# A searched list order that knows PSUM banks, and a prefetch hint for the last branch, in a fused linear-attention and gated-MLP kernel

## The chip, the cores and the metric

The kernel runs on one core of one Trainium2 chip. The time is device microseconds of one execution of the whole kernel, the median of three runs. Engines are named as in the profile: PE (matrix products; PEld is its weight load), DVE, ACT, POOL, and SP, which here only issues transfers.

## What is computed

The reference is a linear attention with decaying state, followed by a gated MLP with spatial mixing, all in float32, with B=4, H=8, S=768, D=48:

```python
for t in range(S):                                     # attention
    cur = einsum('bhd,bhe->bhde', u[None] * kt, vt)
    y[:, :, t] = einsum('bhd,bhde->bhe', rt, state + cur)
    state = wt[:, :, :, None] * state + einsum('bhd,bhe->bhde', kt, vt)
x = y.transpose(0, 2, 1, 3).reshape(B, S, H * D)       # 4 x 768 x 384
h = gelu(x @ w_in)                                     # tanh form
u, v = h[..., :512], h[..., 512:]
v_n = (v - mean(v)) / sqrt(var(v) + 1e-6) * g_ln
v_s = einsum('ts,bsd->btd', w_sg, v_n) + b_sg[None, :, None]
return x + (u * v_s) @ w_out
```

## The kernel before

The sequence is cut into 24 chunks, four batches of six chunks of 128 steps. For each chunk the kernel scans the decays on DVE (lines 635 to 650), scales the keys (`decayed_k`, 652 and 679), forms the weights of a step's own key (`own_weights`, 691 to 717, whose last part is a group of eight ACT rows at L715 or one product at L717 on DVE or POOL), takes scores on PE into the PSUM bank pair `a_ps` (L740), masks them (`masked`, L817), advances the state (`state`, 831 to 847; `decayed`, four ACT rows at L858 or one product at L860) and gathers the outputs in the PSUM pair `y_ps` (763, 774). `taken` then copies two parts of `y_ps` out: three heads' worth into `x` (128x384) and the fourth into `y` (128x128), both through the helper `copy` at L446, on ACT or on DVE; `move` (L982) sends the `y` rows to their place in `x` by three transfers on SP's queue; `split_x` turns `x` on PE (1003, 1004) and splits it into a high and a low part (`xT`). Most products are run as three, high by high, high by low, low by high (L1014 to L1016).

The MLP runs in pieces of the same work: `v_piece` and `u_piece` (x @ w_in, gelu at L1037 and L1070, layernorm 1039 to 1056), `gate_piece` (spatial mixing with `wsgh`, `wsgl` and 1092 to 1098) and `out_piece` (L1116, with the store at L1118). Weights are loaded and split by `f64_weight` (1158 to 1188) and `f32_weight` (1206 to 1212). The first gate product can only start when all six v pieces of a batch are done, some 75 us into the run; before that, chunks and weight work fill PE. Where PE would be idle early, matmuls on unused data are put in (`warm` and `fill`, L551).

All this is written as procedures that yield an operation at a time. A class `Plan` simulates the engines in Python, with a cost in microseconds for each operation, picks what comes next on which engine, and the kernel emits instructions in that order. What it picks is steered by tables of numbers (`LEAD`, `FIRST`, `PIECE`, `WEIGHT`, `BIAS`, `TOL`, `SHIFT`, `LEAN`, `AHEAD`): a rank for each call of each procedure, and a lean to one engine. An operation's earliest start is the latest of its inputs, its buffers, its engine, and a port shared by DVE and POOL. The emitted order is fixed; on the chip each engine runs its own list and waits on semaphores.

At the end a flag that the checks of range have written is read on each engine (L1292), and `with tc.If(flag > 0)` (L1294) holds a general, slower path, which does not run on these inputs: each engine branches over it. L1464 is the end of the function.

Of the kernel before, what the change touches and what calls it, by code (L numbers as in the profile page):

```python
# [36 lines left out]
LEAD = (12.4645, -2.59387, -4.21285, -7.90312)  # L37
FIRST = {"v": -1.41961, "u": 28.6546, "gate": 10.0262, "out": 26.6142}
PIECE = {"v": -16.9089, "u": 12.3224, "gate": 14.337, "out": 5.856}
WEIGHT = {"v": -13.2274, "u": -50.6824, "sg0": -3.39001, "sg1": -8.4941, "out": 2.71291}  # L40

BIAS = {"DVE": 0.278468, "POOL": 0.125302}
TOL = {"ACT": 0.187321, "DVE": 0.0774238, "PE": 0.0750297, "POOL": 0.0114098, "SP": 0.02}
OWN = {"ACT": 0.12, "DVE": 0.12, "PE": 0.0, "POOL": 0.1}
SHIFT = {
    "f64_weight": {1: -2.65682, 2: -0.0161277, 3: 0.0312938, 4: 7.52904, 5: 8.2742, 6: 0.872807, 7: 2.80997,
        8: 0.987471, 9: 2.80075},
    "f64_check": {0: 0.144801, 1: -0.144084, 2: -0.567729, 3: -0.298354, 4: -0.901301, 5: -0.796411, 6: -1.40305,
        7: -4.54019, 8: -6.21746, 9: -2.35678},
    "range_check": {0: -5.99366, 1: -1.89263, 2: -3.53632, 3: -4.15958, 4: -3.59754, 5: -3.76383, 6: -6.85461,  # L50
        7: -7.08113, 8: -3.31642, 9: -10.4712, 10: -2.92299, 11: 0.109737},
    "f32_weight": {0: -3.99499, 1: -0.0910659, 2: 0.252904, 3: -0.00610032, 4: 0.827835, 5: -1.04847},
    "columns": {0: 0.0800858},
    "consts": {0: -1.42278},
    "load_kr": {0: -0.357877, 1: -0.588202, 2: -0.327565, 3: 0.576721, 4: -0.213968, 5: 0.282151, 6: 0.072508,
        7: -0.109793, 8: -0.0751895, 9: -0.848467, 10: -0.0803527, 11: 0.123607, 13: -1.36602, 14: -1.37566,
        15: -1.37566, 16: -0.255794, 17: -0.423447, 18: 0.00265044, 19: 1.42131, 20: 0.396438, 21: 2.56083,
        22: 4.00369, 23: 0.995513},
    "load_v": {0: 2.55696, 1: 0.24433, 2: 0.29339, 3: -3.53162, 4: -0.539967, 5: 1.43151, 6: 1.21722, 7: 1.33442,
        8: -0.963013, 9: 0.685624, 10: 0.16795, 11: -0.752937, 12: 0.336987, 13: 0.680041, 14: 1.11277,  # L60
        15: -0.819155, 16: 0.412499, 17: 0.652678, 18: -4.10874, 19: -1.39921, 20: -0.196712, 21: -2.95851,
        22: -0.225999, 23: -0.122174},
    "decays": {0: 0.290652, 1: 3.36975, 2: -0.337977, 3: 0.287929, 4: -0.550312, 5: -0.458788, 6: -0.107544,
        8: 0.186735, 9: -0.131388, 10: -0.076173, 11: 0.0119462, 12: 2.29576, 13: 6.35672, 14: 0.74578, 15: 4.6382,
        16: 0.256563, 17: 0.173431, 18: -7.30487, 19: -4.8291, 20: -1.76844, 21: -5.70158, 22: -1.11423,
        23: 0.554462},
    "decayed_k": {0: -1.94935, 1: -0.0499885, 2: -3.469, 3: -4.52965, 4: 1.46376, 5: 1.08007, 6: 1.74482,
        7: 1.82159, 8: -6.25161, 9: 0.461373, 10: -0.258781, 11: -1.05508, 12: 0.0573206, 13: 6.34316,
        14: 0.0715837, 15: -3.39515, 16: -0.550587, 17: 3.31994, 18: 2.03045, 19: 1.63861, 20: 2.50708,
        21: 3.49938, 22: 0.149994, 23: -5.18727},  # L70
    "own_weights": {0: -0.99264, 1: -2.30837, 2: -1.40861, 3: 0.124313, 4: 0.939737, 5: 1.08277, 6: 0.689459,
        7: 0.194852, 8: -0.0430578, 9: 1.36362, 10: 0.628226, 11: 1.72692, 12: 0.453539, 13: 1.31489, 14: 0.36321,
        15: 0.326257, 16: 0.527571, 17: -1.51186, 18: -1.02775, 19: -0.416129, 20: -0.985823, 21: 0.0128711,
        22: 0.414581, 23: 0.751683},
# [12 lines left out]
    "turned": {0: -0.36366, 1: 7.62663, 2: 4.98126, 3: 0.412257, 4: 1.31616, 5: 1.44751, 6: -1.90445, 7: -1.89447},
    "scores": {0: -9.60454, 1: -1.60519, 2: 0.00907207, 3: -1.402, 4: -0.278773, 5: -0.377053, 6: -3.00215,
        7: 0.568393},
    "products": {0: 2.53405, 1: -0.218746, 2: 0.641708, 3: 0.0789209, 4: -0.63387, 5: -1.14758, 6: -2.83415},  # L90
    "outputs": {0: 0.272463, 1: 3.35994, 2: -4.09238, 3: 0.997477, 4: -1.80195, 5: -7.63104},
    "load_w": {1: 0.0390948, 2: -0.314065, 3: 0.528507, 4: -0.0361462, 5: 0.0962989, 6: 0.034904, 7: -0.126869,
        8: -0.418661, 9: -0.623567, 10: -0.635585, 11: -0.171762, 12: 1.00086, 13: 0.0732159, 14: -0.722859,
        15: 2.58094, 16: 0.428369, 17: 1.08119, 18: -0.528971, 19: -0.94875, 20: 0.553405, 21: -0.75299,
        22: 0.915889, 23: 15.5269},
    "chunk_pc": {1: -0.0918095, 2: -1.12188, 3: 0.970453, 4: 3.354, 5: 4.35453, 6: -0.563074, 7: -3.79915,
        8: -4.75251, 9: -4.09779, 10: 0.477875, 11: 3.14907, 12: -3.58171, 13: -2.32428, 14: -1.81168,
        15: 0.960833, 16: 1.60902, 17: -0.319454, 18: -6.14497, 19: -0.652345, 20: -4.72639, 21: -0.537364,
# [72 lines left out]
STRETCH = 6  # L171
# [31 lines left out]
class Op:  # L203
# [11 lines left out]
    def port(self, e):  # L215

        return e == "POOL" or e == "DVE" and self.two


class Event:  # L220
    t = None


class Buf:


    def __init__(self, pool, slot):
# [30 lines left out]
class Plan:  # L258
# [55 lines left out]
    def run(self):  # L314
        while True:
            best = {}
            for p in self.procs:
                op = p[3]
# [18 lines left out]
            op = p[3]  # L337
# [1131 lines left out]
```

## Time and profile before

| what | us |
|---|---|
| median of 3 runs | 361.82 (361.63 to 362.58) |
| profiled execution, its own time | 360.56 |
| span of its trace | 358.7 |
| outside the span | 1.86 |

| engine | busy us | share of the span | instructions |
|---|---|---|---|
| PE | 348.8 | 97% | 4495 |
| DVE | 269.5 | 75% | 556 |
| ACT | 208.2 | 58% | 524 |
| POOL | 93.6 | 26% | 154 |

A line of the profile names the line of the kernel, the engine, the operation, what it writes and reads, and the number of such instructions; then the busy time and the mean of one in ns; then how long the engine was idle just before them, and who ended that. One line of code can stand for several engines, as the planner chose. A gap on an engine counts for the whole only where the work that ends last comes through it.

### The profile page before, as it was taken

Reading aid. Unit: us, or ns where it says so; the run is one execution under the profiler, and the core shown is the slowest. Engines: PE = TensorE matmul, PEld = TensorE weight load, DVE = VectorE, ACT = ScalarE, POOL = GpSimd, SP = SyncE. Lnnn points to the kernel's source line nnn. Section 1 sums busy time; section 2 is a strip of 40 time slices with the busy share of each in tenths; the row PEclk is TensorE's granted clock in tenths of the full one; section 3 lists DMA queues with packets and bytes.
Section 4 is the critical chain, followed back from the end, with each engine's and each line's share of the span. In section 5 each row is a group of like instructions: output and inputs, shape, how many; then the busy total and the mean of one; then the engine's idle time right before and its main releaser. Section 6 shows DMA issues by size and latency. Waiting matters only on the chain.

```text
span 358.7 us, 10925 instructions
## 1 busy us (share of the span) xinstructions
PE 348.8 (97%) x4495; PEld 320.4 (89%) x4495; DVE 269.5 (75%) x556; ACT 208.2 (58%) x524; POOL 93.6 (26%) x154
## 2 busy tenths in 40 slices
PE   8998999999999999999999999999999999999993
PEld 7785777899999899899999988999999989999993
DVE  7999999999999989899659879977550425472341
ACT  2769768782535787571214355862467999994110
POOL 8352323214224321224245233231300221100000
PEclk9999999999999999999999999999999999999999
DMA  7989795720465646253277432330487844431002
GB/s 267 372 254 336 238 324 146 232 84 21 145 222 149 221 146 193 92 151 114 62 225 237 149 108 59 126 107 5 152 244 263 289 122 119 132 115 44 24 2 73
DMA packets 26697, 57.06 MB, mean 159 GB/s; under 512 B 3216, under 2 KB 12176, under 8 KB 26640
## 3 DMA queue, kind: packets, MB, share of 16 engines
q1 hardware_dynamic: 26640, 56.29, 49.6%
q8 instruction: 37, 0.61, 0.7%
q14 instruction: 20, 0.16, 0.2%
HBM read 50.37 MB, written 4.72 MB: 154 GB/s over the span
## 4 chain that ended last, share of the span: by engine, by line
PE 85%; DVE 7%; DMA 3%; ACT 1%; issue 1%; SPq 1%; DVEq 0%; ACTq 0%
PE m_ps L1014 19%; PE m_ps L1015 17%; PE m_ps L1016 17%; PE resets L1014 6%; PE resets L1015 5%; PE resets L1016 5%; PE a_ps L740 5%; PE y_ps L763 4%; PE y_ps L774 3%; DMA x<-y 2%; PE y_ps L747 2%; DVE vn L1165 1%; DVE W L635 1%; DVE winl L1171 1%; DVE W L643 1%
## 5 line engine op out<-in xcount | busy, mean ns | idle before, releaser
L1014 PE MATMUL m_ps<-wsgh,vn 128*128 128x384 f32 x144 | 49.5, 344 | 0.0
L1015 PE MATMUL m_ps<-wsgl,vn 128*128 128x384 f32 x144 | 48.7, 338 | 0.0
L1016 PE MATMUL m_ps<-wsgh,vn 128*128 128x384 f32 x144 | 48.7, 338 | 0.0
L1045 POOL TENSOR_TENSOR st<-st,mhalf 128x1 f32<-128x1 f32 x24 | 13.6, 568 | 58.9 <-DVE st L1039 13.4
L1096 ACT CAST g<-m_ps 128x384 fp32r<-128x384 f32 x24 | 11.4, 479 | 29.4 <-DVE m_ps L1094 29.2
L1014 PEld LDWEIGHTS m_ps<-wsgh,vn 128*128 128x128 f32 x144 | 27.0, 188 | 0.6
L1015 PEld LDWEIGHTS m_ps<-wsgl,vn 128*128 128x128 f32 x144 | 27.1, 188 | 0.1
L1016 PEld LDWEIGHTS m_ps<-wsgh,vn 128*128 128x128 f32 x144 | 27.1, 188 | 0.0
L1014 PE MATMUL m_ps<-g,wouth 128*128 128x384 f32 (+1 forms) x80 | 27.0, 337 | 0.0
L1092 DVE SCALAR_TENSOR_TENSOR m_ps<-m_ps,flat 128x384 f32<-128x384 f32 x24 | 14.7, 620 | 15.9 <-PE m_ps L1016 15.8
L1015 PE MATMUL m_ps<-g,wouth 128*128 128x384 f32 (+1 forms) x80 | 26.6, 332 | 0.0
L1016 PE MATMUL m_ps<-g,woutl 128*128 128x384 f32 (+1 forms) x80 | 26.6, 332 | 0.0
L1014 PE MATMUL m_ps<-xT,winh 128*128 128x384 f32 x75 | 26.2, 349 | 0.0
L1015 PE MATMUL m_ps<-xT,winh 128*128 128x384 f32 x75 | 25.4, 338 | 0.0
L1016 PE MATMUL m_ps<-xT,winl 128*128 128x384 f32 x75 | 25.4, 338 | 0.0
L446 ACT COPY x<-y_ps 128x384 f32<-128x384 f32 x21 | 10.0, 478 | 24.3 <-PE y_ps L763 23.8
L1014 PE MATMUL m_ps<-winh,xT 128*128 128x512 f32 x57 | 23.5, 411 | 0.1
L740 PE MATMUL a_ps<-KR 64*64 64x128 f32 (+1 forms) x768 | 22.4, 252 | 1.1 <-DVE S L847 1.0
L1015 PE MATMUL m_ps<-winl,xT 128*128 128x512 f32 x57 | 22.6, 396 | 0.0
L1016 PE MATMUL m_ps<-winh,xT 128*128 128x512 f32 x57 | 22.6, 396 | 0.0
L704 POOL TENSOR_TENSOR RK<-RK,flat 128x384 f32<-128x384 f32 x14 | 14.1, 1010 | 29.8 <-DVE W L635 5.3
L763 PE MATMUL y_ps<-a,vtok 64*64 64x64 f32 x768 | 21.5, 224 | 0.3 <-DMA vtok<-in_vtok 0.2
(195 smaller groups left out, 1014.0 us busy)
## 6 DMA issues: line engine op xcount, KB each, us to landing
KR<-in_kr SPq DMA_DIRECT2D x24, 512.0 KB, 4.8
RK<-in_ktok SPq DMA_DIRECT2D x20, 384.0 KB, 4.3
W<-in_wpad SPq DMA_DIRECT2D x24, 260.5 KB, 3.9
KR<-in_wpad SPq DMA_DIRECT2D x12, 521.0 KB, 3.8
vtok<-in_vtok SPq DMA_DIRECT2D x24, 192.0 KB, 3.7
out<-o SPq DMA_DIRECT2D x21, 192.0 KB, 2.8
vn<-in_w_in SPq DMA_DIRECT2D x6, 512.0 KB, 5.7
KR<-in_w_in SPq DMA_DIRECT2D x6, 512.0 KB, 4.2
```

The lines of the kernel that those rows point to most:

```text
L446: nc.scalar.copy(o, i) if e == "ACT" else engine[e].tensor_copy(o, i)
L704: engine[op.e].tensor_tensor(t[:, 0], t[:, 0], u_bc, ALU.mult)
L740: nc.tensor.matmul(ps_[64 * c_:64 * c_ + 64, j, p * C:p * C + (2 * T if c_ < turn else T)], x.K[rows, at:at + T], r_, start=True, stop=True)
L747: m = behind(m, nc.tensor.matmul(at(c_)[64 * j:64 * j + 64, p // 2, p % 2], x.kt.tile[64 * c_:64 * c_ + 64, j, p * 64:(p + 1) * 64], x.V[6 ...
L763: m = nc.tensor.matmul(place(y, j, q, r, c_), x.V[64 * c_:64 * c_ + 64, h * D - up(p, j):h * D - up(p, j) + 64], x.a.tile[64 * c_:64 * c_ ...
L774: m = behind(m, nc.tensor.matmul(place(y, j, q, r, c_), S2.tile[64 * j:64 * j + 64, 16 + 64 * p - up(p, j):80 + 64 * p - up(p, j)], x.R[64 ...
L1014: nc.tensor.matmul(ps, lh, rh, start=(i == 0), stop=False)
L1015: nc.tensor.matmul(ps, lh, rl, start=False, stop=False)
L1016: nc.tensor.matmul(ps, ll, rh, start=False, stop=(i == n - 1))
L1045: nc.gpsimd.tensor_tensor(rstd, var, c.mhalf, ALU.pow)
L1092: nc.vector.scalar_tensor_tensor(ps, ps, c.g[:, d:d + 1], c.b_bc[:, ts], ALU.mult, ALU.add)
L1096: nc.scalar.copy(gh, ps)
```

## The change

Three things are changed in the planner and one at the end of the kernel.

First, the planner knows a `Bank`: an operation that names banks may not start before every other engine's last access to them has ended. The copies of `taken`, the mask, the state's additions, the copy of the scores' turned part and a small look at `y_ps` name the banks that they read. Second, some costs are set anew (own weights on PE, state and decayed on POOL and ACT, the small layernorm steps on POOL). Third, every number of the tables is another one. Fourth, a hint for the branch at L1294 is asked for on all five engines. Lines after it move by up to 24; L446 becomes L462, L982 becomes L1003, L1294 becomes L1318.

```diff
-    "state": {0: 1.17605, 1: -1.5654, 2: -0.151852, 4: -1.00713, 5: -1.43132, 6: 0.034972, 7: 0.148255,
+    "state": {0: 1.6156, 1: -1.5654, 2: -0.151852, 4: -1.00713, 5: -1.43132, 6: 0.0152658, 7: 0.148255,
...
+class Bank:
+
+
+    def __init__(self):
+        self.t = {}
+
+    def since(self, e):
+        return max((t for k, t in self.t.items() if k != e), default=0.0)
...
-                                            self.lanes[0] if op.kb is not None else 0.0),))
+                                            self.lanes[0] if op.kb is not None else 0.0,
+                                            *(b.since(e) for b in op.banks)),))
...
+            for b in op.banks:
+                b.t[e] = op.seen
...
+    for n, x in enumerate(ch):
+        x.yb, x.ab = ([Bank(), Bank()] for _ in range(2))
+        x.db = ch[n - 1].yb if n > STRETCH else [Bank(), Bank()]
...
-            op = yield Op({"PE": 1.0}, small=True, after=[e_uc], take=[m_m], free=[rk], n=16)
+            op = yield Op({"PE": 1.3}, small=True, after=[e_uc], take=[m_m], free=[rk], n=16)
...
-        op = yield Op({"DVE": 0.64}, after=[x.e_A, x.e_Sc], done=x.e_M)
+        op = yield Op({"DVE": 0.64}, after=[x.e_A, x.e_Sc], done=x.e_M, banks=x.ab)
...
-            op = yield Op({"DVE": 0.27}, after=[x.e_Ds, x.e_S2], take=[s_S1])
+            op = yield Op({"DVE": 0.27}, after=[x.e_Ds, x.e_S2], take=[s_S1], banks=x.db[:1])
...
-        op = yield Op({"DVE": 0.3, "POOL": 0.6, "ACT": 1.0}, after=[before.e_S1, x.e_pc], take=[s_S2], done=x.e_S2,
+        op = yield Op({"DVE": 0.3, "POOL": 0.49, "ACT": 0.95}, after=[before.e_S1, x.e_pc], take=[s_S2], done=x.e_S2,
...
-        op = yield Op({"ACT": 0.42, "DVE": 0.47}, after=[x.e_ym], take=[s_x] if first else [], apart=True)
+        op = yield Op({"ACT": 0.42, "DVE": 0.47}, after=[x.e_ym], take=[s_x] if first else [], apart=True,
+                      banks=x.yb)
...
-        op = yield Op({"ACT": 0.19, "DVE": 0.22}, take=[s_y3] if first else [], free=[y], apart=True)
+        op = yield Op({"ACT": 0.19, "DVE": 0.22}, take=[s_y3] if first else [], free=[y], apart=True,
+                      banks=x.yb[1:])
...
-        yield Op({"POOL": 0.7})
+        yield Op({"POOL": 0.55})
...
+    tc.mark_branch_hint_location(
+        "general", hint="LikelyTaken",
+        engines=[x.engine for x in (nc.sync, nc.vector, nc.tensor, nc.scalar, nc.gpsimd)])
     flag = nc.values_load(bad[0:1, 0:1], min_val=0, max_val=1)
     fast.close()
-    with tc.If(flag > 0):
+    with tc.If(flag > 0, label="general"):
```

What this makes of the order is seen at three places. The first is the start of SP's list, before and after (`W`, `KR` and `u_col` are the first loads).

```order
L1464 UNCONDITIONAL_BRANCH
L600 DMA W_0_81<-in_wpad 128x521
L609 DMA KR_0_83<-in_kr 128x1024
L1217 DMA u_col<-in_ucol 128x32
L600 DMA W_0_82<-in_wpad 128x521
L609 DMA KR_0_84<-in_kr 128x1024
```

```order
L1488 UNCONDITIONAL_BRANCH
L1488 BRANCH_PREFETCH_HINT
L619 DMA W_0_81<-in_wpad 128x521
L628 DMA KR_0_83<-in_kr 128x1024
L619 DMA W_0_82<-in_wpad 128x521
L1238 DMA u_col<-in_ucol 128x32
L628 DMA KR_0_84<-in_kr 128x1024
```

One hint instruction stands right behind the branch into the kernel, on this and in the same way on each of the other four engines; there is none near L1318, where the branch is.

The second place is the fourth chunk's copies out of `y_ps`, some 42 us into the run. On ACT before and then on DVE before (`x_0_111` and `y_0_114` are the two parts of `taken`, `S` the states):

```order
L446 COPY kt_0_103<-m_ps_0_134 128x512
L1037 ACTIVATE v_0_126,st_0_115<-m_ps_0_133 128x512
L446 COPY x_0_111<-y_ps_0_131 128x3x128
L446 COPY pc_0_97<-W_0_82 128x8
L858 ACTIVATE S_0_109<-S_0_104,pc_0_96 128x48 x4
L446 CAST xT_539<-x_0_110 128x3x128
```

```order
L847 TENSOR_TENSOR S_0_104<-a_ps_0_130,S_0_108 128x192
L446 COPY y_0_114<-y_ps_0_131 128x128
L641 RECIPROCAL resets<-W_0_82 128x4
L679 TENSOR_TENSOR KR_0_84<-KR_0_84,W_0_82 128x512
L652 TENSOR_TENSOR KR_0_83<-KR_0_83,W_0_81 128x512
```

And on ACT after:

```order
L462 COPY pc_0_96<-W_0_81 128x8
L734 ACTIVATE a_0_101<-KR_0_83,own_0_92 128x64 x8
L462 CAST wsgh<-g_572 128x2x384
L462 COPY look_0_95<-y_ps_0_131 128x1
L462 COPY kt_0_103<-m_ps_0_133 128x512
L462 COPY pc_0_97<-W_0_82 128x8
L1058 ACTIVATE v_0_126,st_0_115<-m_ps_0_134 128x512
L462 CAST xT_555<-x_0_110 128x3x128
L1062 ACTIVATE junk,st_0_115<-v_0_126,st_0_115 128x512
L462 COPY x_0_111<-y_ps_0_131 128x3x128
L462 COPY y_0_114<-y_ps_0_131 128x128
L877 ACTIVATE S_0_109<-S_0_104,pc_0_96 128x48 x4
```

Both copies of the chunk now stand one behind the other on ACT, and a group of eight L734 rows (L715 of before) stands ahead of them; over the whole run ACT takes all 24 pairs, where DVE took 12 of the `y` copies and 3 of the `x` copies.

The third place is SP's list around the fourth chunk's move (`g` are parts of the mixing weight), before and after:

```order
L982 DMA x_0_110<-y_0_113 32x128 x3
L1206 DMA g_725<-in_w_sgT 128x2x384
L1206 DMA g_727<-in_w_sgT 128x2x384
L609 DMA KR_0_85<-in_kr 128x1024
L609 DMA KR_0_86<-in_kr 128x1024
L617 DMA vtok_0_87<-in_vtok 128x384
L982 DMA x_0_111<-y_0_114 32x128 x3
```

```order
L1003 DMA x_0_110<-y_0_113 32x128 x3
L642 DMA RK_0_91<-in_ktok 128x768
L1227 DMA g_724<-in_w_sgT 128x2x384
L1227 DMA g_731<-in_w_sgT 128x2x384
L1227 DMA g_737<-in_w_sgT 128x2x384
L642 DMA RK_0_90<-in_ktok 128x768
L636 DMA vtok_0_87<-in_vtok 128x384
L628 DMA KR_0_86<-in_kr 128x1024
L1003 DMA x_0_111<-y_0_114 32x128 x3
```

Seven loads instead of five stand between the third move and the fourth.

Counted over each list up to the first gate product, PE has 6 more u products, 16 more scores and 3 fewer fillers, and the rest alike; DVE has 148 rows for 150, ACT 162 for 130, POOL 66 for 59. Of DVE's, one more set of a weight's split (four rows, less one of another set), two more L1052, one L652, one L679 and one L709 come; two L717, one L706, one L840 and six small rows go. Of ACT's, two groups of eight L715, three groups of four L858, three L1070 and one L1041 come, two L1050 go. Over the whole run ACT has 136 L715 rows for 80.

## Rows read from the trace of the kernel before

**Rows 1.** The page: busy time, share and instructions of each engine.

```profile
PE 348.8 (97%) x4495; PEld 320.4 (89%) x4495; DVE 269.5 (75%) x556; ACT 208.2 (58%) x524; POOL 93.6 (26%) x154
```

**Rows 2.** Windows before and behind the first gate product: stretch, its length, then busy times.

```profile
core 0: us, PE busy (x) PEld busy (x) DVE busy (x) ACT busy (x) POOL busy (x), PEclk, DMA share, GB/s
0.00:75.00 75.00, 71.16 (x1081) 57.16 (x1082) 71.25 (x155) 53.29 (x145) 29.12 (x63) 1.00 0.79 260
75.00:345.80 270.80, 270.34 (x3366) 256.15 (x3364) 194.69 (x394) 154.46 (x379) 64.46 (x91) 1.00 0.44 136
```

**Rows 3.** Waits of PE: line <- releaser: us in total, times, longest.

```profile
PE m_ps L551 <- POOL junk L528: 1.2, 1, 1.2
PE a_ps L740 <- DVE S L847: 1.0, 1, 1.0
...
PE m_ps L1003 <- ACT u L1070: 0.4, 1, 0.4
```

**Rows 4.** The chain that ended last, in order of time: start, us, what.

```profile
46.18 5.11 DMA x<-y
...
53.01 0.91 PE m_ps L1003 x2
...
99.84 0.88 PE a_ps L740 x32
```

**Rows 5.** Timeline of the last 6 us: start, us, engine, line, [idle <-releaser].

```profile
353.13 0.36 DVE L1116 TENSOR_TENSOR u<-m_ps,x 128x192 f32<-128x192 f32 x1 [0.76 <-PE m_ps L1016]
353.52 0.46 SPq L1118 DMA_DIRECT2D out<-u  x1
```

**Rows 6.** Transfers issued from 350 us on: KB each, median us to landing.

```profile
out<-u SPq DMA_DIRECT2D x2, 96.0 KB, 1.7
```

**Rows 7.** Instructions of L1294: queue, count, ns min/median/max, first to last start.

```profile
L1294 SPq EVENT_SEMAPHORE  x8: 17/17/17, 356.7 to 357.3; - x8
...
L1294 ACTq COMPARE_BRANCH  x1: 50/50/50, 347.7 to 347.7; - x1
L1294 ACTq EVENT_SEMAPHORE  x1: 17/17/17, 348.2 to 348.2; - x1
L1294 PEldq COMPARE_BRANCH  x1: 3842/3842/3842, 351.2 to 351.2; - x1
...
L1294 SPq COMPARE_BRANCH  x1: 50/50/50, 354.0 to 354.0; - x1
```

**Rows 8.** Timeline: two matmuls of 384 columns in a row on PE.

```profile
345.02 0.34 PE L1016 MATMUL m_ps<-wsgh,vn 128*128 128x384 f32 x1
345.19 0.34 PE L1014 MATMUL m_ps<-wsgh,vn 128*128 128x384 f32 x1
```

**Rows 9.** Groups of instructions by line and shape: busy us, mean ns | idle before.

```profile
L715 ACT ACTIVATE a<-KR,own 128x64 f32<-128x64 f32 x80 | 20.2, 338 | 1.0 <-DVE own L709 0.9
...
L679 DVE TENSOR_TENSOR KR<-KR,W 128x512 f32<-128x512 f32 x22 | 15.8, 721 | 0.2 <-DMA KR<-in_kr 0.2
...
L652 DVE TENSOR_TENSOR KR<-KR,W 128x512 f32<-128x512 f32 x17 | 12.6, 742 | 0.0
...
L858 ACT ACTIVATE S<-S,pc 128x48 f32<-128x48 f32 x40 | 10.1, 324 | 2.3 <-DVE S L847 2.2
...
L1052 DVE TENSOR_SCALAR v<-v,st 128x512 f32<-128x512 f32 x9 | 4.9, 547 | 0.7 <-POOL st L1047 0.5
...
L717 DVE TENSOR_TENSOR a<-own,KR 128x512 f32<-128x512 f32 x7 | 4.8, 679 | 0.0
...
L446 DVE COPY y<-y_ps 128x128 f32<-128x128 f32 x12 | 3.5, 290 | 12.8 <-ACT x L446 12.8
...
L1043 DVE TENSOR_SCALAR st<-st 128x1 f32<-128x1 f32 x22 | 3.1, 142 | 4.5 <-ACT junk L1041 4.5
...
L1165 DVE SCALAR_TENSOR_TENSOR g<-g,g 128x384 int32<-128x384 int32 x4 | 2.1, 555 | 0.0
...
L1163 DVE TENSOR_SCALAR g<-g 128x384 int32<-128x384 int32 x4 | 1.3, 352 | 0.0
```

More of the change, by code (lines that the diff above doesn't have):

```diff
@@ L34 @@
 WMID, WHALF = 1.11, 0.48
[L37 to L43, printed above, removed]
+LEAD = (12.2642, -2.6384, -4.06392, -10.5789)
+FIRST = {"v": -1.82498, "u": 25.5999, "gate": 6.37033, "out": 27.5547}
@@ L44 @@
+PIECE = {"v": -20.0832, "u": 13.1418, "gate": 16.1515, "out": 12.0275}
+WEIGHT = {"v": -13.2138, "u": -47.5409, "sg0": -1.91549, "sg1": -20.2575, "out": 4.3844}
+BIAS = {"DVE": 0.351334, "POOL": 0.115945}
+TOL = {"ACT": 0.147636, "DVE": 0.0774238, "PE": 0.0629901, "POOL": 0.0642896, "SP": 0.02}
 OWN = {"ACT": 0.12, "DVE": 0.12, "PE": 0.0, "POOL": 0.1}
 SHIFT = {
-    "f64_weight": {1: -2.65682, 2: -0.0161277, 3: 0.0312938, 4: 7.52904, 5: 8.2742, 6: 0.872807, 7: 2.80997,
-        8: 0.987471, 9: 2.80075},
@@ L48 @@
[L48 to L62, printed above, removed]
@@ L172 @@
 RESETS = 8
[L173 to L174 removed]
+AHEAD = {"decays": -0.692084, "decayed_k": -8.62155, "own_weights": 13.6876, "masked": -2.18884, "state": 0.2945,
+         "decayed": 21.3635, "taken": -34.7049, "stretch": -4.83707, "move": -5.22689, "split_x": -0.281107}
 HMIN = float.fromhex("0x1.2p-15")
@@ L203, with __init__ @@
 class Op:
-    def __init__(self, on, after=(), take=(), free=(), done=None, kb=None, two=False, apart=False, small=False, slack=0.0, n=6):
+    def __init__(self, on, after=(), take=(), free=(), done=None, kb=None, two=False, apart=False, small=False, slack=0.0, n=6,
+                 banks=()):
         self.on, self.after, self.take, self.free, self.done, self.kb = on, after, take, free, done, kb
         self.two = two
+        self.banks = banks
         self.n = n
@@ L831, in state @@
             nc.vector.tensor_tensor(two(S1.tile), x.ds_at(0), two(values(x.S2.tile)), ALU.add)
-        op = yield Op({"DVE": 0.3, "POOL": 0.6} if g else {"DVE": 0.3}, after=[x.e_Ds, x.e_pc], take=[s_S2], done=x.e_T2,
-                      two=g > 0)
+        op = yield Op({"DVE": 0.3, "POOL": 0.49} if g else {"DVE": 0.3}, after=[x.e_Ds, x.e_pc], take=[s_S2], done=x.e_T2,
+                      two=g > 0, banks=[] if g else x.db[:1])
         (S1 if g else x.ds).done(op.seen)
@@ L842, in state @@
         if not last:
-            op = yield Op({"DVE": 0.27}, take=[s_S1], done=x.e_S1)
+            op = yield Op({"DVE": 0.27}, take=[s_S1], done=x.e_S1, banks=x.db[1:])
             x.S1, = op.got
@@ L873, in outputs @@
         pe_own(x, y, True)
-        op = yield Op({"ACT": 0.1, "DVE": 0.1}, take=[s_look])
+        op = yield Op({"ACT": 0.1, "DVE": 0.1}, take=[s_look], banks=x.yb[:1])
         look, = op.got
@@ L935, in turned_copy @@
         m = T if last_of(n) else C
-        op = yield Op({"ACT": 0.5, "DVE": 0.61}, after=[x.e_T], take=[s_kt], done=x.e_kt)
+        op = yield Op({"ACT": 0.5, "DVE": 0.61}, after=[x.e_T], take=[s_kt], done=x.e_kt, banks=x.ab)
         x.kt, = op.got
@@ L1037, in v_piece @@
         nc.scalar.activation(v, m.tile, AF.Gelu_apprx_tanh, accum_out=neg)
-        op = yield Op({"POOL": 0.3, "DVE": 0.08}, two=True)
+        op = yield Op({"POOL": 0.2, "DVE": 0.08}, two=True)
         engine[op.e].tensor_scalar(neg, neg, -1.0 / FF, None, ALU.mult)
```

196 lines of the change are left out of this document (106 added, 90 removed), and 16 rows, old and new, of the table SHIFT.

## The prediction

> **What bounds the kernel now.** I read the shares of the page first, then the windows, then PE's waits, and only then the chain and the end. PE is busy for 348.8 of 358.7 us, 97% [rows 1], so the whole is PE's work plus the little that PE is idle. The windows say where that little lies [rows 2]: from 75 us, when the first gate product starts, to 345.8 us PE is busy 270.34 of 270.80 us, and in the first 75 us it is busy 71.16, idle 3.84. Whatever an order can win without taking work from PE is therefore in the head, and is at most 3.84 us. PE's longest waits agree: 1.2 us at the very start for data that POOL writes, 1.0 for a state on DVE, 0.4 for a gelu on ACT [rows 3]. In the head DVE is busy 71.25 of 75 us and ACT 53.29 [rows 2]: DVE, not PE, is the fullest engine there, and ACT has 21.7 us to spare. The chain that ended last goes once through a transfer, 5.11 us from 46.18, and is back on PE at 53.01 [rows 4]; this is the fourth chunk's move of `y` into `x`.
>
> The end is a place of its own. The last add on DVE starts at 353.13, the last store is issued at 353.52 [rows 5], and a store of this size lands 1.7 us after its issue [rows 6], so at about 355.2. But SP, which takes its branch at 354.0 in 50 ns, runs its next instruction at L1294 only at 356.7 [rows 7]: 2.7 us later, some 1.5 behind the store's landing. ACT's branch stands at 347.7 and its next instruction at 348.2, 0.45 us later; PE's own branch record is 3.84 us long [rows 7], but it starts at 351.2, and ends at 355.05, ahead of SP. So the branch over the general path costs an engine between some 0.45 and 3.8 us, and on SP it is what ends last. What lies behind it in the span is 358.7 less 356.7, 2.0 us, and stays.
>
> **The change part by part.** *The banks.* Of DVE's waits the largest that a bank order could end is that of the 12 `y` copies, 12.8 us in all, all for the `x` copy on ACT [rows 9]. From the code, the two read the same PSUM pair. With both copies on ACT that wait is gone, and ACT takes the 12 copies at about the 0.29 us that DVE had: 3.5 us over the whole run on an engine that is idle for 358.7 less 208.2 us [rows 1]. PE's list of waits has none for one of these copies, and behind 75 us PE is idle for 0.46 us in all [rows 2]. So nearly all of the 12.8 us were beside PE's work, and I cost the bank part at nothing; what hides it is the dense PE of the second window, and if that cover were gone PE would show idle time there.
>
> *The order of the head.* Ahead of the first gate product PE now does 6 more u products and 16 more scores. Two products of 384 columns follow each other by 0.175 us (345.02 to 345.19) [rows 8], so six are 1.05 us; 16 scores are one piece of 0.88 us [rows 4] (each stands twice in the trace). That is 1.93 us of work that fits into the head and need not be done later. The 3 fillers fewer have no price, since they stand only where PE is idle. Against this stands DVE, the fullest engine of the head, whose list up to that product changes as follows [rows 9]. It gains a weight set less one of its rows (0.352 and twice 0.555: 1.46), two L1052 (1.09), an L679 and an L652 (1.46) and a reduction of 384 columns at the 0.555 of the like-sized L1165 (0.56): 4.57 us. It loses two L717 (1.36), one product of 384 columns (0.56), one state product of 192 columns, which I put at the 0.29 of the `y` copy, and six small rows, between 0.142 and 0.29 each: 0.85 to 1.74, middle 1.30: in all 3.51. DVE's net is +1.06 us, and 0.6 to 1.5 by the bounds. If DVE sets the first gate product's time, that product comes 1.06 us later with 1.93 us more behind it: **-0.87 us, I take -0.8**. By DVE's bounds it is -0.4 to -1.3; if DVE's added rows all fall into its own 3.75 us of idle, -1.9; the ceiling is PE's 3.84.
>
> *The fourth move.* Seven loads instead of five stand between the third move and the fourth on SP's queue. An issue takes SP 0.46 us [rows 5], so two more in front of it are up to 0.9 us, on a chain that passes through this move [rows 4]; the PE work between that chunk's end and the product that the move feeds is shorter by a u triple as well. This is a part of the upper bound of the order and not of its middle, since the copies ahead of it are ordered anew as well.
>
> *The smaller costs* (own weights, state, small POOL rows) change no instruction's time; they act through the order alone and are in the counts above.
>
> *The hint.* It adds one instruction on each engine at the start. The nearest rows, control instructions at L1294, take 17 to 50 ns [rows 7]; SP's first load stands behind it, so +0.05, and up to 0.2 if it holds its queue for four of them. What it may win is at the end: if the code behind the branch is there, SP needs only the landing of the last store. From 356.7 to 355.2 that is **-1.5 us**. Bounds: 0 if the hint does nothing; -1.5 if all engines follow, because then the landing is next in line; between them, since DVE's and PE's branches end at about the same time as SP's, a part. I take -1.5, since the ACT row shows that 0.45 us is enough for a branch on this kernel, which from 354.0 would be before the landing.
>
> [...]
>
> The sum: -0.8 + 0.05 - 1.5 = -2.25 us. Against the profiled execution (358.7 in the span and 1.86 outside of it, 360.56) that is 358.3; the median of the runs stands 1.26 above that execution, and the prediction is for a median: 361.82 - 2.25 = 359.6 (**A**).
>
> **The rivals.** *B: the hint does nothing.* It stands some 350 us ahead of the branch; thousands of instructions run between on PE (4495 rows [rows 1]). Then SP's 2.7 us stay: 361.82 - 0.8 + 0.05 = 361.1. For it: the place of the hint in the order. Against: five instructions that name a branch by its label may hold its place and act when it comes near, and nothing in the trace of before tells. In the same family, a hint that brings code in at a bad time could cost a fetch at the start, priced at PE's 3.84 us [rows 7]: 361.82 - 0.8 + 3.84 = 364.9; I give that little.
>
> *C: ACT becomes the head's bound, and the kernel is slower.* ACT's list ahead of the first gate product grows from 130 to 162 rows. Two groups of eight L715 come at 8 x 0.2525 (20.2 us over 80 rows) = 2.0 us each, three groups of four L858 at 4 x 0.2525 (10.1 over 40) = 1.0 us each [rows 9], so some 7 us and the copies. ACT's 21.7 us of room [rows 2] hide them as long as none stands ahead of a row that PE is waiting for. The place is in the order: a group of L734 now stands three to eight rows ahead of the fourth chunk's copies, and PE already waits 0.4 us for an ACT row in the head [rows 3]. One group in front of one such row costs 2.0 us and decides the head as soon as DVE's list is not later than it: 361.82 + 2.0 + 0.05 - 1.5 = 362.4 with the hint, 363.9 without it. Against it: 21.7 us of room is a lot for 7.
>
> *E: the order takes all of PE's idle time out of the head*, and the hint works: 361.82 - 3.84 - 1.5 + 0.05 = 356.5. For it: a searched order that has 1.93 us more PE work early. Against: 1.2 us of the waits are at the very start, before any data is there.
>
> **How the numbers follow.** Chances: A 0.48, B 0.25, C 0.16 (half of it with the hint), E 0.09, harm by the hint 0.02. The likeliest is A, 359.6. Its own range, by the order's -1.9 to -0.4 and the hint's -1.5 to -0.9, is 358.4 to 360.6. The range of eight in ten reaches to B and to the first of C's times: 357.4 (A's low end less 1 us for a head that is part of the way to E) to 363.0 (C's 362.4 and half a us); left out are E, C without the hint and the harm, 0.19. A measurement of this kernel tells a difference from none at about 0.3%, 1.1 us, so faster is below 360.7 and slower above 362.9. Faster: A and E less a small part of A's upper end, 0.54. Same: B, C with the hint, and that part, 0.36. Slower: C without the hint and the harm, 0.10.
>
> **What would show it.** In the changed kernel's windows, PE's idle time up to the first gate product should be 3 us or less, with the first gate product near 76 us, and behind it PE dense as now. The DVE wait for the `x` copy should be gone without a change of PE's idle time behind the head; if PE's second window gains, the cover that I named was not one. At L1294, SP's next instruction should come about 1.2 us after its branch (the landing) rather than 2.7; if it is still 2.7 the hint is B. PE's branch record, now 3.84 us, should be short if the hint acts on PE. An ACT row in front of a long PE wait in the head would be C. I am wrong altogether if the end is not SP's branch but the runtime's work behind it, or if PE's matmuls themselves change their spacing.

## The result and the profile after

The changed kernel took 357.87 us (357.33 to 358.74, 4 runs) against 361.75 us (361.63 to 362.58, 4 runs) for the kernel before beside it: a ratio of 0.989, 95% interval 0.9864 to 0.9916, or -3.9 us. Forecast were 359.6 us and -2.25. The profiled execution of the changed kernel took 358.19 us, of which the trace spans 356.5; against 360.56 and 358.7 before that is -2.4 and -2.2. Two later series, on two chips and with more runs, gave smaller gains than the first comparison: 0.9954 (0.9936 to 0.9973) and 0.9937 (0.9915 to 0.996), -1.4 and -2.5 us between the medians. The kernel before had 360.03 (35 runs) and 360.75 us (34 runs) there.

The windows of the changed kernel, up to 75 us, on to the last stretch, and the last stretch of PE's work, to be read beside [rows 2] (PEclk is the granted clock, 1.00 for full speed):

```profile
core 0: us, PE busy (x) PEld busy (x) DVE busy (x) ACT busy (x) POOL busy (x), PEclk, DMA share, GB/s
0.00:75.00 75.00, 70.76 (x1075) 56.53 (x1076) 70.56 (x141) 56.88 (x170) 32.87 (x70) 1.00 0.80 266
75.00:345.00 270.00, 269.67 (x3366) 255.71 (x3364) 186.13 (x350) 162.03 (x417) 77.00 (x123) 1.00 0.44 135
345.00:352.30 7.30, 7.29 (x51) 7.08 (x50) 3.17 (x7) 0.48 (x1) 0.00 (x0) 1.00 0.14 46
```

PE's idle time in the head is 4.24 us, where it was 3.84 [rows 2]; behind it PE is as dense as it was. PE's waits, to be read beside [rows 3] (line <- releaser: us, times, longest):

```profile
PE m_ps L567 <- POOL junk L544: 1.3, 1, 1.3
PE m_ps L715 <- POOL RK L710: 0.7, 1, 0.7
PE m_ps L1196 <- ACT winl L462: 0.7, 1, 0.7
```

The 1.0 us for a state on DVE is gone, and a wait of 0.7 us for ACT has come. DVE's `y` copies, which waited 12.8 us for ACT [rows 9], stand on ACT now, and a state's addition on DVE waits for them instead:

```profile
DVE S L850 <- ACT y L462: 7.2, 6, 4.2
```

The timeline of the end, beside [rows 5]:

```profile
352.02 0.27 PE L1037 MATMUL m_ps<-g,woutl 128*128 128x192 f32 x1
352.32 0.36 DVE L1137 TENSOR_TENSOR u<-m_ps,x 128x192 f32<-128x192 f32 x1 [0.76 <-PE m_ps L1037]
352.71 0.53 SPq L1139 DMA_DIRECT2D out<-u  x1
```

The last add starts at 352.32 instead of 353.13, 0.81 us earlier. And the branch, L1318 now, beside [rows 7] (queue, count, ns min/median/max, first to last start):

```profile
L1318 SPq EVENT_SEMAPHORE  x8: 17/17/17, 354.5 to 355.1; - x8
...
L1318 ACTq COMPARE_BRANCH  x1: 68/68/68, 347.0 to 347.0; - x1
L1318 ACTq EVENT_SEMAPHORE  x1: 17/17/17, 347.5 to 347.5; - x1
L1318 PEldq COMPARE_BRANCH  x1: 398/398/398, 350.4 to 350.4; - x1
...
L1318 SPq COMPARE_BRANCH  x1: 70/70/70, 353.3 to 353.3; - x1
```

SP runs on 1.2 us after its branch, at 354.5, which is the store's issue at 352.71 plus 1.8 to its landing; before it was 2.7. PE's branch record is 0.40 us long and was 3.84. From the last add's start to the end of the span it is 356.5 - 352.32 = 4.2 us, and was 358.7 - 353.13 = 5.6: 1.4 us less. The hint instructions at the start took 45 to 56 ns on each engine.

### The profile page after: what moved, and what is told of

It reads as the page before. It is cut to its first block, busy times and chain, and to the rows that moved or that the text cites. A ratio compares the mean times of both kernels' runs of the same rounds, so it can differ in the third digit from the quotient of the medians.

```text
span 356.5 us, 10996 instructions
## 1 busy us (share of the span) xinstructions
PE 347.7 (98%) x4489; PEld 319.3 (90%) x4489; DVE 260.2 (73%) x498; ACT 219.4 (62%) x586; POOL 109.9 (31%) x193
## 4 chain that ended last, share of the span: by engine, by line
PE 87%; ACT 2%; DVE 1%; DMA 1%; issue 0%; SPq 0%; ACTq 0%
PE m_ps L1035 19%; PE m_ps L1037 18%; PE m_ps L1036 18%; PE resets L1035 6%; PE resets L1036 5%; PE resets L1037 5%; PE a_ps L759 5%; PE y_ps L782 4%; PE y_ps L793 3%; PE y_ps L766 2%; DMA x<-y 1%; PE m_ps L1024 1%; PE a_ps L766 1%; ACT a L734 1%; PE m_ps L805 0%
## 5 line engine op out<-in xcount | busy, mean ns | idle before, releaser
L1035 PE MATMUL m_ps<-wsgh,vn 128*128 128x384 f32 x156 | 53.7, 344 | 0.0
L1037 PE MATMUL m_ps<-wsgh,vn 128*128 128x384 f32 x156 | 52.7, 338 | 0.0
L1036 PE MATMUL m_ps<-wsgl,vn 128*128 128x384 f32 x156 | 52.7, 338 | 0.0
L734 ACT ACTIVATE a<-KR,own 128x64 f32<-128x64 f32 x136 | 34.4, 339 | 2.9 <-DVE own L728 2.8
L1035 PEld LDWEIGHTS m_ps<-wsgh,vn 128*128 128x128 f32 x156 | 29.3, 188 | 0.6
L1036 PEld LDWEIGHTS m_ps<-wsgl,vn 128*128 128x128 f32 x156 | 29.3, 188 | 0.0
L1037 PEld LDWEIGHTS m_ps<-wsgh,vn 128*128 128x128 f32 x156 | 29.3, 188 | 0.0
L462 ACT COPY x<-y_ps 128x384 f32<-128x384 f32 x24 | 11.4, 476 | 24.3 <-PE y_ps L782 20.0
L1077 DVE TENSOR_TENSOR vn<-v,vn 128x512 fp32r<-128x512 f32 x24 | 16.9, 706 | 12.3 <-ACT vn L462 10.1
L1035 PE MATMUL m_ps<-xT,winh 128*128 128x384 f32 x69 | 24.3, 352 | 0.0
L1035 PE MATMUL m_ps<-g,wouth 128*128 128x384 f32 (+1 forms) x72 | 24.2, 336 | 0.0
L1036 PE MATMUL m_ps<-g,wouth 128*128 128x384 f32 (+1 forms) x72 | 23.9, 332 | 0.0
L1037 PE MATMUL m_ps<-g,woutl 128*128 128x384 f32 (+1 forms) x72 | 23.8, 331 | 0.0
L725 POOL TENSOR_TENSOR RK<-RK 128x384 f32<-128x384 f32 x16 | 16.1, 1009 | 24.7 <-DVE W L669 6.1
L1036 PE MATMUL m_ps<-xT,winh 128*128 128x384 f32 x69 | 23.3, 338 | 0.0
```

What stands on the lines that cost most here:

```text
L462: nc.scalar.copy(o, i) if e == "ACT" else engine[e].tensor_copy(o, i)
L725: engine[op.e].tensor_tensor(t[:, 1], t[:, 1], t[:, 0], ALU.mult)
L734: nc.scalar.activation(a[:, j, p], eyes, AF.Copy, scale=o[:, j, p:p + 1])
L1035: nc.tensor.matmul(ps, lh, rh, start=(i == 0), stop=False)
L1036: nc.tensor.matmul(ps, lh, rl, start=False, stop=False)
L1037: nc.tensor.matmul(ps, ll, rh, start=False, stop=(i == n - 1))
```

## The experiments

**The hint alone.** The kernel before with the call that asks for the hint, and nothing else of the change:

```diff
+    tc.mark_branch_hint_location(
+        "general", hint="LikelyTaken",
+        engines=[x.engine for x in (nc.sync, nc.vector, nc.tensor, nc.scalar, nc.gpsimd)])
     flag = nc.values_load(bad[0:1, 0:1], min_val=0, max_val=1)
...
-    with tc.If(flag > 0):
+    with tc.If(flag > 0, label="general"):
```

The view of transfers lists those of instructions as a kind of their own, in the trace of before 37 of 16 KB and 20 of 8 KB; a "block" of code in the expectations is such a piece.

> The kernel before with the hint for all five engines and nothing else. My theory: the hint acts although it stands at the start of the program; SP runs its next instruction about 1.2 us after its branch (the last store's landing) instead of 2.7, PE's branch record falls from 3.84 to about 0.4 us, and the time falls by 1.5 us, to 360.2. Rival: the hint alone does nothing and the shorter end of the changed kernel comes from where its code happens to lie in blocks; then 2.7 us stay and the time is 361.7.

Measured: 358.62 us against 360.03, ratio 0.996 (0.9936 to 0.9984). Its instructions at the branch:

```profile
L1297 SPq EVENT_SEMAPHORE  x8: 17/17/17, 355.6 to 356.2; - x8
...
L1297 PEldq COMPARE_BRANCH  x1: 393/393/393, 351.5 to 351.5; - x1
...
L1297 SPq COMPARE_BRANCH  x1: 70/70/70, 354.4 to 354.4; - x1
```

1.2 us on SP, 0.39 on PE: the hint acts, without any help of the new order, although it stands at the program's start. A second series beside the changed kernel:

> The kernel before with the hint alone, a second time, now beside the changed kernel in one series. In the first series both had 358.62 us, so the order had nothing left to give beside the hint. If that holds: within 0.4 us of the changed kernel, and 1.4 us below the kernel before. Rival: the first comparison of all, 3.9 us for both parts together, is the truer one; then the changed kernel is 2 us or more below this one.

> The changed kernel, a second time: 1.4 to 1.7 us below the kernel before if the first series holds, 3.9 if the first comparison does. By the theory that the order is worth 0.5 at most: within 0.4 us of the hint alone.

Measured: 359.20 us for the hint alone and 358.25 for the changed kernel, against 360.75: ratios 0.9952 (0.9925 to 0.9979) and 0.9937 (0.9915 to 0.996). In the first series the two were equal:

> The changed kernel once more, beside the others on one chip. If the 3.9 us hold: 357.9. If the profiled pair (2.4 us) is nearer to the truth: 359.3.

Measured: 358.62 us, the same median as with the hint alone. So by the medians the hint is worth 1.4 and 1.55 us in the two series, and the order beside it 0 and 0.95. The intervals of the two kernels overlap in both series, so the order's part beside the hint is not told apart from nothing.

**The order alone.** The changed kernel without the two lines of the hint:

```diff
-    tc.mark_branch_hint_location(
...
-    with tc.If(flag > 0, label="general"):
+    with tc.If(flag > 0):
```

> The changed kernel without the hint: the new order alone. The last product ended 0.8 us earlier in the changed kernel's trace than before, so by the traces the order is worth 0.8: 360.9. Rival: by the medians of the runs the change is worth 3.9, of which the hint can have 1.5, so the order is worth 2.4: 359.4. In either case SP's 2.7 us at the branch should be back if the hint was the cause.

Measured: 359.70 us against 360.03, ratio 0.9987 (0.9964 to 1.0009). The time of the branch is back:

```profile
L1315 SPq EVENT_SEMAPHORE  x8: 17/17/17, 355.7 to 356.3; - x8
...
L1315 PEldq COMPARE_BRANCH  x1: 4022/4022/4022, 350.0 to 350.0; - x1
...
L1315 SPq COMPARE_BRANCH  x1: 50/50/50, 353.0 to 353.0; - x1
```

The order alone is not told apart from nothing. Its middle, -0.3 to -0.5 us, is smaller than the forecast -0.8, which still lies inside the interval (-1.3 to +0.3 us); the rival of -2.4 falls.

**Which engine's branch it is.** The kernel before with the hint on fewer engines:

```diff
-        engines=[x.engine for x in (nc.sync, nc.vector, nc.tensor, nc.scalar, nc.gpsimd)])
+        engines=[x.engine for x in (nc.sync, nc.vector)])
```

> The kernel before with the hint on SP and DVE alone. These two were the last to run on behind their branch (356.7 and 356.9), PE was at 355.1, ahead of the last store's landing at 355.2. My theory: the whole 1.5 us come from these two: 360.2, with PE's branch still 3.84 us long. Rival: PE's missing block holds up the end as soon as the other two are early: 361.0 or more.

Measured: 359.11 against 360.03, ratio 0.997 (0.9949 to 0.9992). PE's branch record is 3.50 us long there, SP runs on 1.2 us after its own, and the trace ends 4.0 us after the last product, as it does with all five (4.0 and 4.1). With `(nc.sync,)` alone:

> The kernel before with the hint on SP alone. DVE, without it, runs on only 356.9 us into the run, behind SP's 356.7 of before. If the end waits for all engines, nothing is won: 361.7, with SP's wait short and DVE's long. Rival: SP's store wait is what ends last and DVE's part is hidden: 360.2.

Measured: 360.05 against 360.58, ratio 0.9987 (0.9962 to 1.0011). DVE is the last now:

```profile
L1297 SPq EVENT_SEMAPHORE  x8: 17/17/17, 357.1 to 357.6; - x8
...
L1297 DVEq COMPARE_BRANCH  x1: 72/72/72, 355.7 to 355.7; - x1
L1297 SPq COMPARE_BRANCH  x1: 70/70/70, 355.8 to 355.8; - x1
...
L1297 DVEq EVENT_SEMAPHORE  x1: 21/21/21, 358.6 to 358.6; - x1
```

SP runs on 1.3 us after its branch, DVE 2.9 after its own, and the end waits for it. The trace ends 4.7 us after the last product: a part of the 1.5 is won, not nothing, as I had written, and not all. The kernel before shows the same row on DVE, behind SP's 356.7 of [rows 7]:

```profile
L1294 DVEq EVENT_SEMAPHORE  x1: 21/21/21, 356.9 to 356.9; - x1
```

The end needs both engines, and PE's long branch is hidden. That SP and DVE win all of it, and SP a part, is read from the ends of the traces, one of each; the runs' -0.9 and -0.5 us go the same way, but do not tell these two apart, and the second is not told from nothing.

**The copies.** The kernel before with the DVE's 12 `y` copies on ACT:

```diff
-        copy(op.e, half.y3.tile[:, cs], y.tile[:, 1, 1, 0:C])
+        copy("ACT", half.y3.tile[:, cs], y.tile[:, 1, 1, 0:C])
```

> The kernel before with the 12 y copies that stood on DVE put on ACT, at the same place of the emitted order. Takes away the 12.8 us of DVE's waits for ACT's x copy and gives ACT 12 x 0.29 = 3.5 us. My theory: all of it lies beside PE's work; 361.7, within 0.5. Rival: a part of the 12.8 us holds up PE through DVE's later rows in the head (one of the ten lies there): 360.7 or less; or the copies hold ACT's rows that PE waits for: 362.5 or more.

Measured: 360.32 against 360.58, ratio 1.0002 (0.9968 to 1.0036). DVE's waits for ACT's copies in it:

```profile
DVE S L831 <- ACT y L446: 5.6, 7, 2.0
DVE S L831 <- ACT x L446: 0.7, 1, 0.7
```

The 12.8 us of [rows 9] are gone; the state's addition, which reads `y_ps` as well, now waits 5.6 us for ACT's `y` copies (the 0.7 us for an `x` copy are in the trace of before too). Neither reaches PE.

**The tables of before in the planner of after** (banks, costs and hint as in the changed kernel, all number tables as before):

> The changed kernel (banks, costs, hint) planned with the tables of before. The tables were searched for a planner without banks; with banks in the planner every later choice shifts. My theory: tables and planner belong together, and the old tables give a worse order than either kernel: some 2 to 6 us above the changed kernel, 360 to 364. Rival: the banks and costs alone carry the gain and the tables none: 358 to 359.

Measured: 382.15 against 360.58, ratio 1.0581 (1.0553 to 1.061): worse than I had thought possible. Its PE waits 6.2 us at one place. The view of waits names no releaser for it ("issue"), but PE's queue has one semaphore row of 6.53 us there, from 95.40 to 101.93, which waits for DVE among others, and the last row to end before it is DVE's mask, which reads the scores' bank pair `a_ps`, of which there is one:

```profile
L758 PEldq EVENT_SEMAPHORE  x15: 51/51/6534, 14.0 to 280.8; - x15
```

```profile
101.17 0.71 DVE L835 COPY_PREDICATED a<-mask,a_ps 128x512 f32<-128x512 uint8 x1
```

So this reads as a wait for data: with the old tables the mask comes late, and PE stands until it is done. In the windows around this wait (start to end, length, PE busy first, PEclk is the third number from the right) the clock changes:

```profile
94.00:96.00 2.00, 1.83 (x25) 1.45 (x23) 2.00 (x7) 0.91 (x3) 0.00 (x0) 1.00 0.76 235
96.00:98.00 2.00, 0.00 (x0) 0.00 (x0) 2.00 (x6) 1.61 (x6) 0.27 (x1) 1.00 0.59 183
98.00:100.00 2.00, 0.00 (x0) 0.00 (x0) 2.00 (x4) 0.00 (x0) 0.91 (x1) 0.53 0.03 9
100.00:104.00 4.00, 2.02 (x44) 2.05 (x48) 4.00 (x8) 0.20 (x1) 1.05 (x1) 0.50 0.80 263
```

So a new order was needed with the banks, and the tables are a part of one design with the planner's rules. (The section on the change calls every number of the tables another one; some are the same in both, the second of `state`, -1.5654, among them.)

**Where the order's gain lies.** The first gate product starts later in the changed kernel. On PE's timeline before and after:

```profile
74.94 0.34 PE L1014 MATMUL m_ps<-wsgh,vn 128*128 128x384 f32 x1
```

```profile
76.75 0.44 PE L1035 MATMUL m_ps<-wsgh,vn 128*128 128x384 f32 x1
```

It is 1.81 us later, with the 1.93 us more of PE work in front of it that the prediction counted: the head gained 0.1. Other traces agree: where the clock stays up in the head, the order before has this product at 74.6 to 75.0 us (four traces), the new order at 76.0 to 77.2 (four without added products). From there to the last product's end it is 353.09 - 74.94 = 278.15 us before and 352.29 - 76.75 = 275.54 after, 2.61 less, of which 1.93 is that work: 0.7 us were won behind the head, where I had looked for nothing.

A part of that has a place. In the order before, in the second trace of the hint alone, the chain of waits reads (start, us, what):

```profile
106.29 0.88 PE a_ps L740 x32
107.16 0.45 PE y_ps L747 x32
107.61 0.48 PE y_ps L774 x32
108.09 0.12 PE y_ps L763 x8
108.21 1.16 issue
109.37 0.34 PE y_ps L763 x5
```

In the middle of a group of 16 like products PE stops for 1.16 us and nothing releases it. Of six traces with PE's order of before (four of them with a hint, one with the copies on ACT), four show a stop at this very product: by the distance between two starts, less the usual one, 0.33 us in two (the kernel before itself, at 108.7, is one), 0.88 and 1.36. Five traces with the new order have none there. Such a stop fits a wait for code: it stands in a dense stretch of small products, and in the middle of a group, where no instruction has a semaphore to wait for. The traces can say more. They hold transfers of instructions (37 of 16 KB in the trace of before, one for some 245 of PE's 9060 records). In the four traces with the stop, PE goes on 1.36 to 1.47 us after the last of these has landed. That transfer landed 0.03, 0.5, 1.0 and 1.1 us before PE came to the place where the stop is 1.36, 0.88, 0.33 and 0.33 us, and 1.4 and 1.7 us before in the two traces without a stop. So the stop is a wait for code, and its size follows from how late the transfer is. Less the stop, the stretch from the first gate product to the end of the last product takes 277.7 to 277.9 us in all six, and 275.5 to 275.9 in the new order; less the 1.93 us of work, that leaves some 0.3 of the 0.7 without a place. The two experiments below, made for another question, bear on the stop as well.

**Fillers at 9 us.** In two traces of the order before with a hint the granted clock falls early. The windows of the hint alone, first trace:

```profile
9.00:10.50 1.50, 1.09 (x11) 0.90 (x9) 1.38 (x4) 1.50 (x6) 1.50 (x2) 1.00 1.01 374
10.50:12.00 1.50, 1.44 (x36) 1.23 (x36) 1.30 (x3) 1.47 (x8) 0.34 (x2) 0.53 1.00 365
12.00:14.00 2.00, 2.00 (x10) 2.00 (x11) 1.90 (x4) 1.76 (x8) 1.13 (x1) 0.50 1.06 418
14.00:16.00 2.00, 1.95 (x59) 1.57 (x58) 1.16 (x4) 0.49 (x2) 0.00 (x0) 1.00 1.02 400
```

PEclk is 0.53 and 0.50 between 10.5 and 14 us. Before it, PE waited 0.4 us for POOL; in the other trace, that of the hint on SP alone, it waited 0.9 and PEclk is 0.50 from 12.5 to 15.5 us. In the kernel before the same wait is 0.6 us; the prediction's list of PE's longest waits (1.2, 1.0, 0.4) leaves it out:

```profile
PE m_ps L696 <- POOL RK L691: 0.6, 1, 0.6
```

The kernel before with two more fillers at that wait, and a second kernel with two tiny products there, which fill less of it but lengthen PE's list by the same two products (with their weight loads, eight records of the trace):

```diff
-            warm(ident, 2, m.tile)
+            warm(ident, 4 if n == 1 else 2, m.tile)
```

```diff
             warm(ident, 2, m.tile)
+            if n == 1:
+                for _ in range(2):
+                    nc.tensor.matmul(m.tile[:, 0:8], ident, ident[:, 0:8], start=True, stop=True)
```

When the fillers were put in, 16 of 58 executions of the kernel before had a mean clock of 0.994 or less, at a median of 361.8 us against 359.8 for the others; "such a clock" is one of 0.994 or less.

> The kernel before with two more filler products on PE ahead of the second chunk's own weights, at 9 us, where PE stands idle for 0.4 to 0.9 us. [...] Theory: the idle stretch lets the clock fall, so with the fillers no execution, or one, of twelve has such a clock, and the median falls by 0.2 to 0.5 us. Rival: the fall comes from something else (how busy PE is over a longer stretch ahead of it); then the share of such executions stays at a quarter and the time is the same or 0.1 us longer.

> The kernel before with two tiny extra products (8 columns) at the place where the fillers were put at 9 us: PE's list is longer by two instructions from there on, as with the fillers, but PE's idle stretch at 9 us stays nearly as it was. Two theories are tried. One: the stretches in which PE waits for nothing that the trace shows (up to 1.2 us at 109 us in the order before, 0.8 at 40 us with the fillers, none in the changed order) are waits for code, whose place follows from the count of instructions; then the stretch at 109 us is gone and one of about 0.8 us stands at 40 us, as with the fillers. Rival: it is a matter of the moment (a transfer, a lost record); then it may stand at 109 us or nowhere. The other: PE's idle stretch at 9 us lets the clock fall; then a quarter to a half of the executions again have a mean clock of 0.994 or less, where the fillers had none of twelve. Rival: the fillers' shift, not their filling, did it; then none. Time: 360.5 to 361.5.

Measured, fillers: 360.62 against 360.75, ratio 0.9994 (0.9973 to 1.0015), and none of 12 executions with a mean clock of 0.994 or less, where the kernel before beside it had 16 of 34 (these took 360.7 to 362.4 us, the others mostly 359 to 360.6). Measured, tiny products: 360.87 against 360.65, ratio 1.0009 (0.9981 to 1.0036), and 4 of 12 such executions beside 6 of 17. So the fillers go with fewer executions of a low mean clock. That they do it by filling the wait is not shown: the one trace with them still has 0.61 us of it, where the tiny products have 0.73 and the kernel before 0.59. Nor does the length of the wait decide: the clock stayed at 1.00 after 0.9 us in the second trace of the hint alone and after 1.1 in that with SP and DVE. The mean clock is a rough sign besides, since it also counts the time behind the last product, where a low clock costs nothing. The kernel with the order alone has 0.995 in its trace, and the whole of the missing 0.005 lies there, where PE does nothing and PEclk is 0.50:

```profile
353.90:357.60 3.70, 0.00 (x0) 0.00 (x0) 0.00 (x0) 0.00 (x0) 0.00 (x0) 0.50 0.04 13
```

And yet the fillers won no time: with their median of 360.62 they are 0.8 us behind the 18 executions of the kernel before with a mean clock above 0.994, whose median is 359.84. Their chain of waits shows one reason (the chain of the tiny products behind it):

```profile
39.97 0.37 PE m_ps L786 x2
40.34 0.80 issue
41.14 0.44 PE m_ps L786 x2
```

```profile
39.90 0.37 PE m_ps L789 x2
40.27 0.10 issue
40.37 0.44 PE m_ps L789 x2
```

Two more products, and in both kernels a stop appears at 40 us between the same two products, 0.80 us in one execution and 0.10 in the other, while the one at 109 us is down to 0.1. Counted in PE's list of products, weight loads and semaphore rows, the stop at 40 us stands behind record 1217 in both, and the one at 109 us behind record 3265 in all the traces that have it: 2048 apart. So the place follows from the count of PE's records, and between the two places the trace of before has eight transfers of 16 KB, one for 256 records; I read the two as boundaries in the code. Here too PE goes on 1.45 and 1.38 us after the last transfer of instructions has landed. I had forecast the place at 40 us, and missed the size. Behind most of the 37 transfers no such stop is seen; at these two places it is up to 1.36 us.

The changed kernel with the same two fillers:

> The changed kernel with the same two fillers. If the idle stretch at 9 us is what lets the clock fall, its executions are as even as possible and the median is 0 to 0.3 us below the changed kernel; if the fillers come in the way of the own weights, 0.2 us above.

Measured: 358.12 us beside 358.25 without them, ratios 0.9946 (0.9916 to 0.9976) and 0.9937. The fillers are worth nothing there; two of its 12 executions have a mean clock of 0.987 and 0.988 and took 361.65 and 360.60, so two fillers in this one stretch do not keep the clock up in every order.

## Why the prediction was right

**The hint** was right in mechanism, sign and size. The step was: SP's 2.7 us at the branch become the landing's 1.2, so -1.5. The trace shows 1.2. From the last product's end to the end of the span it is 4.0 to 4.2 us in every trace with the hint on SP and DVE, and 5.4 to 5.7 in every one without any, and the runs say 1.4 and 1.55. One reading was incomplete: the prediction took SP for what ends last, and DVE's 356.9 stands behind SP's 356.7; with the hint on SP alone only a part was won. Rival B, that the hint is too far ahead of its branch, falls: the trace shows the branch short, with the hint instruction at 0.8 us and the branch at 353.3. How the chip keeps the hint until then no run here shows. That the branch waits for code was the prediction's assumption, and the transfers agree with it. In the trace of before SP and DVE take their branches at 354.0 and 353.9; two transfers of instructions of 8 KB start at 354.92 and 354.98, land at 355.48 and 355.45, and the two engines run on at 356.7 and 356.9. One of 16 KB lands at 353.59, and PE, at its branch since 351.2, goes on at 355.1. In the changed kernel no transfer of instructions lands between the branches of SP and DVE (353.3 and 353.0) and their next instructions (354.5 and 353.7). The bound between, that a part comes if fewer engines follow, is what the ends of the two partial kernels' traces show: all with SP and DVE, a part with SP alone.

**The banks** at nothing was right, and by the cover that was named: in the kernel of before with the copies on ACT the 12.8 us vanished, 5.6 us of waiting came to the state's addition, and the time did not move.

**The order** came out at its size in the profiled pair by luck. The last product ends 0.8 us earlier there, but as 0.1 in the head and 0.7 behind it, and the runs do not tell the order from nothing. The term was -0.8, made of 1.93 us more PE work in the head against 1.06 us more on DVE. The first gate product came 1.81 us later and not 1.06, so the head gave 0.1 and not 0.87. The step that failed is the one that let DVE's own list set the product's time. In the changed kernel the head's chain passes through ACT instead (start, us, what):

```profile
31.21 1.92 ACT a L734 x8
33.13 0.48 ACT winl L462
33.61 0.04 issue
33.65 1.12 PE m_ps L1196 x2
```

The wait of 0.7 us at this product stands in all five traces of the new order. This is rival C's mechanism, a group of eight rows in front of a row that PE waits for, near its price of 2.0 us (1.92) for the group; but PE's wait for it was 0.7 us, since most of the group lay beside PE's work. C did not decide the time, and it is where a part of the head's gain went. What the order did win lies behind the head, 0.7 us in the profiled pair. There I had put nothing, because PE's idle time in [rows 2] is 0.46 us; but the stop at 109 us in the order before, up to 1.36 us, comes and goes from run to run, and the one profiled execution that I had showed it at 0.33. The other part of the 0.7, some 0.3 to 0.4, has no place that I found. The fourth move's later place on SP and the start's hint cost are not seen.

**The size of the whole.** The first comparison gave -3.9, outside of what the two terms can explain, the later series -1.4 and -2.5, with -2.25 between them. A part of the difference may be the clock in the four runs of before: their 361.6 to 362.6 us are about what the kernel before takes in the later series when its mean clock is 0.994 or less (38 of 109 executions), but the clock of those four is not on record, so this stays open. The kernel's own spread, 3.3 to 4.9 us from the fastest to the slowest execution of before in the four later series, is larger than what the change is worth; I had taken 0.3%, 1.1 us, as enough to tell a difference from none.

What I forecast for the profile and did not come: PE's idle time in the head of 3 us or less (4.24), and rival E with it.

## What to carry to other kernels

Look at what each engine does at its last branch: here SP and DVE ran on 2.7 and 3.0 us after theirs while ACT needed 0.45, and a hint for all engines that end last was worth 1.4 and 1.55 us, on SP alone only a part. A wait on an engine beside a dense PE was worth nothing here, however long the list of waits made it (12.8 us on DVE taken away, ratio 1.0002); and work that is moved ahead of a landmark wins only what the landmark does not move (1.93 us of it put the first gate product 1.81 us later). Two products added to PE's list at 9 us brought a stop of 0.80 and 0.10 us at 40 us, where the order before has none, and left 0.1 of the one at 109 us; compare several executions before an edit of a fraction of a per cent is judged by its own mechanism.

## What the runs showed of the hardware

A prefetch hint given at the start of the program, some 350 us ahead, shortened the branch over the general path on the three engines whose branch is long without it: the record is 393 to 398 ns on PE where it is 3.5 to 4.0 us without; SP runs on 1.2 to 1.3 us after its branch instead of 2.7, DVE 0.6 to 0.7 instead of 2.9 to 3.0. On ACT and POOL that is 0.2 to 0.5 us with it and without. PE stopped for 0.1 to 1.4 us at a place that follows from the count of its instructions (records 1217 and 3265), until 1.36 to 1.47 us after a transfer of instructions has landed. The granted clock of PE fell from 1.00 to 0.50 for some 3.5 us, in two traces of the order before, behind a wait of 0.4 and 0.9 us among sparse small products at 9 us; in others it stayed up after 0.2 to 1.1 us there. With the old tables it fell as well behind a wait of 2.2 at the same place, to a mean of 0.83 between 10 and 20 us. Of the executions of the kernel before, 38 of 109 have a mean clock of 0.994 or less (the two traces have 0.992), at a median of 361.44 us against 359.9 for the others; with two more fillers ahead of that wait none of 12 had. Within the 6.2 us wait in the kernel with the old tables it fell too, to 0.53 and 0.50 from 98 us on. Outside of the span, the kernel before, and those made of it without a hint, took 1.9 us, and the changed order, with the hint and without it, 1.7 to 1.8, as did the order before with a hint; why is not settled.
